# Attention backward on one Trainium2 core: dQ formed inside the loop from dS blocks transposed SBUF to SBUF, and dV with dK in one PSUM tile

## Chip, cores, metric

The kernel runs on one core of one Trainium2 chip. The metric is device time in microseconds, the median of several executions. Profiles are of one execution. Engines are written as in the profile: PE is the TensorE matmul, PEld its weight load, DVE is VectorE, ACT is ScalarE, POOL is GpSimd, SP is SyncE, which here only issues DMAs.

## The reference, cut to what matters

The reference computes a transformer block (2048 tokens, model width 512, 32 heads of width 16, feed-forward width 1792) and its gradients. Only the backward pass of the attention matters here. With E = exp(scores) and dOs, the output gradient divided by the softmax sum, the kernel computes for each head

```
S  = q k^T * 0.25           E  = exp(S)
D  = dOs v^T - delta        dS = E * D            (2048 x 2048 for each head)
dV = E^T dOs                dK = 0.25 * dS^T q
dQ = 0.25 * dS k            <- this one needs dS with k on the partitions
```

In the matmuls of this loop the contracted index lies on the partitions of both operands (psS in the profile: `32*128 32x512`, contracted over the 32 rows of a head). The loop produces dS with the query index on the partitions. That is right for dV and dK, which contract over queries. dQ contracts over keys, so it needs dS transposed.

## The kernel before

Four heads sit in 32-partition strips, so all matmuls of the loop use a part of the array (matmuls of other stages write `128*128` in the profile). psS and psD contract over 32 rows (row-tiled: the profile writes `32*128`). accV and accK contract over 128 rows into 32 columns (column-tiled: `128*32`). A scheduler orders the instructions of each engine at build time, from dependences and a cost model; the program order gives only priorities.

```python
# attention backward loop, cut; 8 head groups x 4 key chunks x 16 query tiles x 2 pairs of heads
for hp2 in range(2):
    psS_u = psu.tile([P, 2, 512], F32, name="psS_u", tag="pu")     # psu: 3 buffers of 128x1024 f32
    for hi in range(2):
        PE.matmul(psS_u[:, hi, :], qt_sb[32*hq:32*hq+32, ...], kt_sb[32*hq:32*hq+32, ...], ..., tile_position=(32*hq, 0))
    ACT.activation(E_u[:], psS_u[:], AF.Exp, scale=SCALE)
    psD_u = psu.tile([P, 2, 512], F32, name="psD_u", tag="pu")
    ...                                                             # psD_u <- dot_sb, vt_sb, row-tiled
    DVE.tensor_tensor(dS_u[:], psD_u[:], E_u[:], ALU.mult)
    for hi in range(2):
        PE.matmul(accV[32*hq:32*hq+32, :], dOs_tokpad[...], E_u[:, hi, :], ..., tile_position=(0, 32*hq))
        PE.matmul(accK[32*hq:32*hq+32, :], q_tok[...], dS_u[:, hi, :], ..., tile_position=(0, 32*hq))
    (POOL if (unit_ctr % 4) != 3 else SP).dma_start(out=dmadst, in_=dS_u[:])   # dS to DRAM
...
# a stage of its own for dQ, after the loop
for kt in range(TT):
    for hq in range(4):
        SP.dma_start(out=rd[:], in_=src, transpose=True)            # 2048 x 128 of dS, 512 KB
    for qc in range(QC):
        for hq in range(4):
            PE.matmul(accs[qc][32*hq:32*hq+32, :], k_tok[...], rds[hq][:, qc*512:(qc+1)*512], ..., tile_position=(0, 32*hq))
```

## Time and profile before

Before, the median is 6780 us (6771 to 6783). The first fence is from the page: busy tenths in 40 equal slices of the span for PE, the clock that TensorE was granted, and the DMA share.

```profile
PE   4799999997937668999999999999998666666676
...
PEclk8755555556968585555555555555555776767687
DMA  2200000001335543232333323232325999999932
```

The next is the table by stretches: length, busy time of each engine with the number of instructions in brackets, granted clock, DMA share and GB/s. The rows are the backward loop, the dQ stage, and the tail.

```profile
core 0: us, PE busy (x) PEld busy (x) DVE busy (x) ACT busy (x) POOL busy (x), PEclk, DMA share, GB/s
2544.00:5180.00 2636.00, 2541.46 (x8192) 443.87 (x8191) 1412.95 (x1280) 1049.99 (x1025) 547.99 (x768) 0.50 0.32 112
5180.00:6420.00 1240.00, 781.49 (x2036) 185.33 (x2037) 17.38 (x28) 0.00 (x0) 0.00 (x0) 0.70 1.18 220
6420.00:6740.00 320.00, 216.16 (x1058) 95.35 (x1075) 165.69 (x463) 28.99 (x52) 0.00 (x0) 0.76 0.25 82
```

In the loop PE is busy 96% of the time, and DVE and ACT about half. The granted clock is half of full speed throughout. In the dQ stage the DMA share is 1.18 (the packets' times add up to more than the span of the 16 engines, so packets overlap in time), and PE waits 461 us in all (478 waits) for transposed reads.

One period of the loop, PE alone, from the timeline. Columns: start, duration, engine, line, operation, tiles, shape, count.

```profile
3501.23 0.63 PE L700 MATMUL psD_u<-iv,ido 32*128 32x512 bf16 x1
3501.79 0.61 PE L711 MATMUL accK<-dS_u,q_tokH 128*32 128x512 bf16 x2
3502.33 0.60 PE L692 MATMUL psS_u<-ik,iq 32*128 32x512 bf16 x1
3502.86 0.61 PE L708 MATMUL accV<-E_u,dOs_tokpad 128*32 128x512 bf16 x2
3503.40 0.60 PE L692 MATMUL psS_u<-ik,iq 32*128 32x512 bf16 x1
3503.41 1.02 PE L700 MATMUL psD_u<-iv,ido 32*128 32x512 bf16 x2
```

Read the starts rather than the durations. Two matmuls on different strips start some 3 ns apart (the `x2` lines last 0.61 us, hardly more than one matmul). Two on the same strip start 0.40 us apart. From a row-tiled to a column-tiled matmul, or back, it takes 0.53 to 0.56 us (3501.23 to 3501.79, 3501.79 to 3502.33).

In what follows a **unit** is four heads, 128 queries, 512 keys; there are 512 units and one took 5.13 us. A **change** is a step between row- and column-tiled matmuls in the built PE order; there were 7.51 of them in a unit.

### The profile page before, as it was taken

The page shows a single profiled execution, that of the slowest core. Times are in us where ns is not written, and L with a number is a line of the kernel's source. Part 1 is how long each engine was busy: PE and PEld are TensorE (multiplying, and loading weights), DVE is VectorE, ACT ScalarE, POOL GpSimd, SP SyncE. Part 2 cuts the span into 40 slices and gives each one's busy share as a digit, 9 for nine tenths or more (in the row PEclk, how much of TensorE's full clock was granted, in tenths as well). Part 3 has the DMA queues.
Part 4 walks back from the last instruction along what each step waited for, and adds up shares of the span by engine and source line. Part 5 has one row for each costly group of instructions (what it writes and reads, how often), then busy time and mean ns, then how long its engine had stood idle before and what let it go on. Part 6 is the DMA issues. An engine that isn't in the chain of part 4 may idle for free. (4 is left out here: it accounts for less than half of the span.)

```text
span 6738.8 us, 51100 instructions
## 1 busy us (share of the span) xinstructions
PE 5556.9 (82%) x18807; PEld 1332.4 (20%) x18885; DVE 2278.3 (34%) x3423; ACT 2156.2 (32%) x2174; POOL 653.7 (10%) x920
## 2 busy tenths in 40 slices
PE   4799999997937668999999999999998666666676
PEld 2222222222313221111111111111111111111132
DVE  8300000006725034555555555555554000000044
ACT  0288888882000003433443433434432000000001
POOL 1000000000000021222222222222221000000000
PEclk8755555556968585555555555555555776767687
DMA  2200000001335543232333323232325999999932
GB/s 92 110 7 7 7 7 7 7 1 63 126 100 138 180 147 120 102 121 103 122 112 109 123 103 122 102 122 103 109 103 144 224 222 218 221 216 223 213 100 82
DMA packets 1327401, 764.37 MB, mean 113 GB/s; under 512 B 1144739, under 2 KB 1238439, under 8 KB 1325485
## 3 DMA queue, kind: packets, MB, share of 16 engines
q1 hardware_dynamic: 1259566, 531.42, 33.2%
q0 software_dynamic: 67584, 229.69, 9.9%
q8 instruction: 147, 2.41, 0.1%
q14 instruction: 104, 0.85, 0.0%
HBM read 126.51 MB, written 353.00 MB: 71 GB/s over the span
## 5 line engine op out<-in xcount | busy, mean ns | idle before, releaser
L704 DVE TENSOR_TENSOR dS_u<-psD_u,E_u 128x1024 bf16<-128x1024 f32 x1024 | 1248.2, 1224 | 1239.6 <-ACT E_u L696 1163.9
L696 ACT ACTIVATE E_u<-psS_u 128x1024 bf16<-128x1024 f32 x1024 | 1048.7, 1024 | 1578.6 <-PE psS_u L692 1578.6
L692 PE MATMUL psS_u<-ik,iq 32*128 32x512 bf16 x2048 | 1140.0, 602 | 31.1 <-ACT E_u L696 21.3
L303 ACT ACTIVATE ET<-psST 128x1024 bf16<-128x1024 f32 x1024 | 1047.1, 1025 | 227.8 <-PE psST L300 225.7
L700 PE MATMUL psD_u<-iv,ido 32*128 32x512 bf16 x2048 | 986.0, 616 | 37.1 <-ACT E_u L696 34.5
L300 PE MATMUL psST<-qt_sb,kt_sb 32*128 32x512 bf16 x2048 | 658.3, 603 | 17.3 <-DMA kt_sb<-KtP 17.3
L307 PE MATMUL oacc<-ET,vaug 128*32 128x512 bf16 x2048 | 625.7, 603 | 46.2 <-ACT ET L303 4.4
L711 PE MATMUL accK<-dS_u,q_tokH 128*32 128x512 bf16 x2048 | 624.6, 607 | 26.6 <-DVE dS_u L704 26.4
L708 PE MATMUL accV<-E_u,dOs_tokpad 128*32 128x512 bf16 x2048 | 599.7, 607 | 4.6
L783 ACT ACTIVATE dh1acc<-pdh_33667 128x512 f32<-128x512 f32 x1 | 0.6, 597 | 1262.5 <-PE pdh_33667 L780 1262.5
L743 PEld LDWEIGHTS <-k_tokI 128*32 128x32 bf16 x2048 | 186.2, 113 | 1065.1 <-issue 1010.8
L310 DVE COPY ostage<-oacc 128x512 f32<-128x512 f32 x32 | 22.1, 691 | 1083.7 <-PE oacc L307 1083.7
L692 PEld LDWEIGHTS <-iq 32*128 32x128 bf16 x2048 | 189.3, 98 | 860.9 <-issue 860.9
L711 PEld LDWEIGHTS <-q_tokH 128*32 128x32 bf16 x2048 | 114.1, 102 | 830.1 <-issue 829.8
L307 PEld LDWEIGHTS <-vaug 128*32 128x32 bf16 x2048 | 151.8, 102 | 466.2 <-issue 437.3
L300 PEld LDWEIGHTS <-kt_sb 32*128 32x128 bf16 x2048 | 111.6, 99 | 477.5 <-issue 477.5
L708 PEld LDWEIGHTS <-dOs_tokpad 128*32 128x32 bf16 x2048 | 110.0, 102 | 422.6 <-issue 420.0
L569 ACT ACTIVATE w1blk<-aw_0_13119 128x512 bf16<-128x512 f32 x1 | 0.6, 597 | 552.6 <-PE aw_0_13119 L565 552.6
L437 POOL MEMSET wT_pad<- 128x12288 bf16 x1 | 10.3, 10338 | 1702.7 <-DMA out_dram<-outq 1702.7
L489 PE MATMUL pds<-gfT,w2T 128*128 128x512 bf16 x219 | 55.5, 406 | 107.5 <-DVE dzT L492 78.8
L700 PEld LDWEIGHTS <-ido 32*128 32x128 bf16 x2048 | 127.4, 104 | 83.3 <-issue 77.2
L263 PE MATMUL ppad<-xn1T,wpadT 128*128 128x512 bf16 x376 | 97.8, 405 | 21.7 <-DVE stagep L266 16.2
(1483 smaller groups left out, 4521.4 us busy)
## 6 DMA issues: line engine op xcount, KB each, us to landing
dzld<-dztok_st POOLq DMA_DIRECT2D x32, 448.0 KB, 3.7
dzld<-dztok_st SPq DMA_DIRECT2D x32, 448.0 KB, 3.5
rT_st<-rT SPq DMA_DIRECT2D x4, 1792.0 KB
rtok_st<-rtok SPq DMA_DIRECT2D x16, 448.0 KB, 2.5
stok_st<-stok SPq DMA_DIRECT2D x16, 448.0 KB
rTb<-rT_st SPq DMA_DIRECT2D x4, 1792.0 KB
rtokb<-rtok_st SPq DMA_DIRECT2D x16, 448.0 KB, 4.1
dztok_st<-dztok SPq DMA_DIRECT2D x16, 448.0 KB
```

What stands on the lines that cost most here:

```text
L263: PE.matmul(pp[:], wpadT[:, ic, which, hg, :], h1T[:, ic, qc * 512:(qc + 1) * 512], start=(ic == 0), stop=(ic == DC - 1))
L300: PE.matmul(ps[:, hi, :], kt_sb[32 * hq:32 * hq + 32, kt * P:(kt + 1) * P], qt_sb[32 * hq:32 * hq + 32, qc * 512:(qc + 1) * 512], start=Tr ...
L303: ACT.activation(ET[:, 2 * pair:2 * pair + 2, :], ps[:], AF.Exp, scale=SCALE)
L307: PE.matmul(oacc[32 * hq:32 * hq + 32, :], lhsT, ET[:, hq, :], start=(kt == 0), stop=(kt == TT - 1), tile_position=(0, 32 * hq), skip_grou ...
L489: PE.matmul(pds[:], w2T[:, oc, fc * P:(fc + 1) * P], gfT[:, oc, qc * 512:(qc + 1) * 512], start=(oc == 0), stop=(oc == DC - 1))
L692: PE.matmul(psS_u[:, hi, :], qt_sb[32 * hq:32 * hq + 32, qt * P:(qt + 1) * P], kt_sb[32 * hq:32 * hq + 32, kb:kb + 512], start=True, stop= ...
L696: ACT.activation(E_u[:], psS_u[:], AF.Exp, scale=SCALE)
L700: PE.matmul(psD_u[:, hi, :], dot_sb[32 * hq:32 * hq + 32, qt * P:(qt + 1) * P], vt_sb[32 * hq:32 * hq + 32, kb:kb + 512], start=True, stop ...
L704: DVE.tensor_tensor(dS_u[:], psD_u[:], E_u[:], ALU.mult)
L708: PE.matmul(accV[32 * hq:32 * hq + 32, :], dOs_tokpad[:, qt, hg, 32 * hq:32 * hq + 32], E_u[:, hi, :], start=(qt == 0), stop=(qt == TT - 1 ...
L711: PE.matmul(accK[32 * hq:32 * hq + 32, :], q_tok[:, qt, h * DH:h * DH + 32], dS_u[:, hi, :], start=(qt == 0), stop=(qt == TT - 1), tile_po ...
L743: PE.matmul(accs[qc][32 * hq:32 * hq + 32, :], k_tok[:, kt, h * DH:h * DH + 32], rds[hq][:, qc * 512:(qc + 1) * 512], start=(kt == 0), sto ...
```

## The change

The intent is to remove the dS round trip through DRAM and the whole dQ stage. A DMA transposes each dS block from SBUF to SBUF. The program order puts dQ nine units later. To make room in PSUM for dQ's accumulator, dV and dK of four heads share one of 128x512 f32 (dV in rows 0 to 15 of a strip, dK in rows 16 to 31), which also lets dK and dV be emitted as groups of four heads.

```diff
+        def transpose_unit(u):
+            hg, qc, kc, qi = units[u]
+            if qi == 0:
+                dqt[hg, qc, kc] = tpool.tile([P, 16, 512], BF, name="dsT", tag="dsT")   # tpool: 2 buffers
+            SP.dma_start(out=dqt[hg, qc, kc][:, :, qi * P:(qi + 1) * P],
+                         in_=bst[u][1].rearrange("p h k -> p (h k)"), transpose=True)
+        def kv_quads(u):
...
+            for hq in range(4):
+                PE.matmul(acc[32 * hq:32 * hq + 32, :], st["qz"][:, qt, hq, :], dS_u[:, hq, :],
+                          start=(qi == 0), stop=False, tile_position=(0, 32 * hq), skip_group_check=True)
+            for hq in range(4):
+                PE.matmul(acc[32 * hq:32 * hq + DH, :], dOs_tok[...], E_u[:, hq, :],
+                          start=False, stop=(qi == 3), tile_position=(0, 32 * hq), skip_group_check=True)
...
+        LAG = 6
+        for u in range(NU + LAG + 4):
+            if u < NU:
+                score_pair(u, 0)            # psS, exp, psD, dS of heads 0, 1
+            if 1 <= u <= NU:
+                kv_quads(u - 1)
+            if u < NU:
+                score_pair(u, 1)            # heads 2, 3
+                transpose_unit(u)
+            v = u - LAG - 3
+            if 0 <= v < NU:
+                dq_quad((hg, qc, kc), qi)   # four matmuls into dqacc
-    (the loop and the dQ stage shown above, and the DRAM tiles of dS)
```

Also: dV and dK are flushed from PSUM every four units and summed in SBUF by ACT and POOL. k and q are scaled beforehand. The tail transposes and multiplies two packed tiles instead of three. x is loaded again for the tail to make room in SBUF.

More of the change, by code (lines that the diff above doesn't have):

```diff
@@ L73 @@
         SP.dma_start(out=auxsel[32 * j + 16:32 * j + 17, :], in_=onesf[0:1, 0:1])
-    x0_tok = persist.tile([P, TT, D], BF, name="x0_tok")
+    x0pool = tc.alloc_tile_pool(name="x0pool", bufs=1, side="right")
+    x0_tok = x0pool.tile([P, TT, D], BF, name="x0_tok")
     SP.dma_start(out=x0_tok[:], in_=x_dram)
@@ L105 @@
     dQtP = dram.tile([HG, P, n], BF, name="dQtP")
-    dKtP = dram.tile([HG, P, n], BF, name="dKtP")
-    dVtP = dram.tile([HG, P, n], BF, name="dVtP")
-    dS_st = [[dram.tile([4, n, 512], BF, name=f"dS_{hg}_{kc4}") for kc4 in range(QC)] for hg in range(HG)]
+    dVKtP = dram.tile([HG, P, n], BF, name="dVKtP")
     with ExitStack() as ph:
@@ L432 @@
     x1pool.release()
+    x0pool.release()
     bwdw = ctx.enter_context(tc.tile_pool(name="bwdw", bufs=1))
-    wT_pad = bwdw.tile([P, 24, D], BF, name="wT_pad")
+    wT_pad = bwdw.tile([P, 16, D], BF, name="wT_pad")
     POOL.memset(wT_pad[:], 0.0)
@@ L460 @@
                     r0 = (hg % 2) * 64 + hq * DH
-                    SP.dma_start(out=wT_pad[32 * hq:32 * hq + DH, t3 * 8 + hg, :], in_=tmpT[r0:r0 + DH, :])
+                    o0 = 32 * hq + (DH if t3 == 1 else 0)
+                    SP.dma_start(out=wT_pad[o0:o0 + DH, (0 if t3 == 0 else 8) + hg, :], in_=tmpT[r0:r0 + DH, :])
         for oc in range(DC):
@@ L590 @@
     qpool = tc.alloc_tile_pool(name="qpool", bufs=1)
-    q_tok = qpool.tile([P, TT, QPAD], BF, name="q_tokH")
-    SP.dma_start(out=q_tok[:], in_=q_st[:])
-    dOs_tokpad = qpool.tile([P, TT, HG, P], BF, name="dOs_tokpad")
+    dOs_tok = qpool.tile([P, TT, D], BF, name="dOs_tok")
+    hpool = tc.alloc_tile_pool(name="hpool", bufs=1)
+    dOs_tokpad = hpool.tile([P, TT, HG, P], BF, name="dOs_tokpad")
     POOL.memset(dOs_tokpad[:], 0.0)
-    hpool = tc.alloc_tile_pool(name="hpool", bufs=1)
     woT = hpool.tile([P, DC, D], BF, name="woT")
@@ L629 @@
                 DVE.tensor_tensor(dst, src, rb, ALU.mult)
+                POOL.tensor_copy(dOs_tok[:, t, :].rearrange("q (g h d) -> q g h d", g=HG, h=4), dst)
                 O_t = wk.tile([P, D], BF, name="O_t", tag="O_t")
@@ L661 @@
     hpool.release()
+    KS_tok = qpool.tile([P, TT, QPAD], BF, name="KS_tok")
+    SP.dma_start(out=KS_tok[:], in_=k_st[:])
+    DVE.tensor_scalar(KS_tok[:], KS_tok[:], SCALE, None, ALU.mult)
+    qz = [qpool.tile([P, TT, 4, 32], BF, name=f"qz{i}") for i in range(2)]
+    for i in range(2):
+        POOL.memset(qz[i][:], 0.0)
     with ExitStack() as ph:
@@ L665 @@
         ework = ph.enter_context(tc.tile_pool(name="phIe", bufs=3))
+        tpool = ph.enter_context(tc.tile_pool(name="phIt", bufs=2))
         stg = ph.enter_context(tc.tile_pool(name="phIg", bufs=2))
@@ L668 @@
         psu = ph.enter_context(tc.tile_pool(name="psIu", bufs=3, space=bass.MemoryType.PSUM))
-        psvk = ph.enter_context(tc.tile_pool(name="psIvk", bufs=1, space=bass.MemoryType.PSUM))
-        unit_ctr = 0
-        for hg in range(HG):
-            qt_sb = strm.tile([P, n], BF, name="iq", tag="iq")
-            SP.dma_start(out=qt_sb[:], in_=QtP[hg])
-            kt_sb = strm.tile([P, n], BF, name="ik", tag="ik")
-            SP.dma_start(out=kt_sb[:], in_=KtP[hg])
-            vt_sb = strm.tile([P, n], BF, name="iv", tag="iv")
-            SP.dma_start(out=vt_sb[:], in_=VtP[hg])
-            dot_sb = strm.tile([P, n], BF, name="ido", tag="ido")
-            SP.dma_start(out=dot_sb[:], in_=dOtP[hg])
-            dVstage = stg.tile([P, n], BF, name="dVstage", tag="dVstage")
-            dKstage = stg.tile([P, n], BF, name="dKstage", tag="dKstage")
-            for kc4 in range(QC):
-                kb = kc4 * 512
-                accV = psvk.tile([P, 512], F32, name="accV", tag="accV")
-                accK = psvk.tile([P, 512], F32, name="accK", tag="accK")
-                for qt in range(TT):
-                    for hp2 in range(2):
-                        hqs = (2 * hp2, 2 * hp2 + 1)
-                        psS_u = psu.tile([P, 2, 512], F32, name="psS_u", tag="pu")
-                        for hi in range(2):
-                            hq = hqs[hi]
-                            PE.matmul(psS_u[:, hi, :], qt_sb[32 * hq:32 * hq + 32, qt * P:(qt + 1) * P],
-                                      kt_sb[32 * hq:32 * hq + 32, kb:kb + 512],
-                                      start=True, stop=True, tile_position=(32 * hq, 0))
-                        E_u = ework.tile([P, 2, 512], BF, name="E_u", tag="E_u")
-                        ACT.activation(E_u[:], psS_u[:], AF.Exp, scale=SCALE)
-                        psD_u = psu.tile([P, 2, 512], F32, name="psD_u", tag="pu")
-                        for hi in range(2):
-                            hq = hqs[hi]
-                            PE.matmul(psD_u[:, hi, :], dot_sb[32 * hq:32 * hq + 32, qt * P:(qt + 1) * P],
-                                      vt_sb[32 * hq:32 * hq + 32, kb:kb + 512],
-                                      start=True, stop=True, tile_position=(32 * hq, 0))
-                        dS_u = ework.tile([P, 2, 512], BF, name="dS_u", tag="dS_u", bufs=6)
-                        DVE.tensor_tensor(dS_u[:], psD_u[:], E_u[:], ALU.mult)
-                        for hi in range(2):
-                            hq = hqs[hi]
-                            h = hg * 4 + hq
-                            PE.matmul(accV[32 * hq:32 * hq + 32, :], dOs_tokpad[:, qt, hg, 32 * hq:32 * hq + 32],
-                                      E_u[:, hi, :], start=(qt == 0), stop=(qt == TT - 1),
-                                      tile_position=(0, 32 * hq), skip_group_check=True)
-                            PE.matmul(accK[32 * hq:32 * hq + 32, :], q_tok[:, qt, h * DH:h * DH + 32],
-                                      dS_u[:, hi, :], start=(qt == 0), stop=(qt == TT - 1),
-                                      tile_position=(0, 32 * hq), skip_group_check=True)
-                        dmadst = dS_st[hg][kc4][2 * hp2:2 * hp2 + 2, qt * P:(qt + 1) * P, :].rearrange("h q k -> q h k")
-                        (POOL if (unit_ctr % 4) != 3 else SP).dma_start(out=dmadst, in_=dS_u[:])
-                        unit_ctr += 1
-                for hq in range(4):
-                    DVE.tensor_copy(dVstage[32 * hq:32 * hq + 32, kb:kb + 512], accV[32 * hq:32 * hq + 32, :])
-                    DVE.tensor_scalar(dKstage[32 * hq:32 * hq + 32, kb:kb + 512], accK[32 * hq:32 * hq + 32, :],
-                                      SCALE, None, ALU.mult)
-            SP.dma_start(out=dVtP[hg], in_=dVstage[:])
-            SP.dma_start(out=dKtP[hg], in_=dKstage[:])
@@ L724 @@
-    with ExitStack() as ph:
-        kpool = ph.enter_context(tc.tile_pool(name="phI2k", bufs=1))
-        io = ph.enter_context(tc.tile_pool(name="phI2io", bufs=8))
-        stg = ph.enter_context(tc.tile_pool(name="phI2s", bufs=2))
-        psq = ph.enter_context(tc.tile_pool(name="psI2", bufs=2, space=bass.MemoryType.PSUM))
-        k_tok = kpool.tile([P, TT, QPAD], BF, name="k_tokI")
-        SP.dma_start(out=k_tok[:], in_=k_st[:])
-        for hg in range(HG):
-            accs = [psq.tile([P, 512], F32, name=f"dqacc{qc}", tag=f"dqacc{qc}") for qc in range(QC)]
-            for kt in range(TT):
-                rds = []
-                for hq in range(4):
-                    rd = io.tile([P, n], BF, name="dsT_rd", tag="dsT_rd")
-                    src = dS_st[hg][kt // 4][hq:hq + 1, :, (kt % 4) * P:(kt % 4 + 1) * P].rearrange("h q k -> (h q) k")
-                    SP.dma_start(out=rd[:], in_=src, transpose=True)
-                    rds.append(rd)
-                for qc in range(QC):
-                    for hq in range(4):
-                        h = hg * 4 + hq
-                        PE.matmul(accs[qc][32 * hq:32 * hq + 32, :], k_tok[:, kt, h * DH:h * DH + 32],
-                                  rds[hq][:, qc * 512:(qc + 1) * 512], start=(kt == 0), stop=(kt == TT - 1),
-                                  tile_position=(0, 32 * hq), skip_group_check=True)
-            dQstage = stg.tile([P, n], BF, name="dQstage", tag="dQstage")
-            for qc in range(QC):
-                DVE.tensor_scalar(dQstage[:, qc * 512:(qc + 1) * 512], accs[qc][:], SCALE, None, ALU.mult)
-            SP.dma_start(out=dQtP[hg], in_=dQstage[:])
@@ new lines, with load_head @@
+        psa = ph.enter_context(tc.tile_pool(name="psIa", bufs=1, space=bass.MemoryType.PSUM))
+        units = [(hg, qc, kc, qi) for hg in range(HG) for qc in range(QC) for kc in range(QC) for qi in range(4)]
+        hst, bst, dqt = {}, {}, {}
+        def load_head(hg):
+            st = {}
+            for key, src in (("q", QtP), ("k", KtP), ("v", VtP), ("do", dOtP)):
+                st[key] = strm.tile([P, n], BF, name=f"i{key}", tag=f"i{key}")
+                SP.dma_start(out=st[key][:], in_=src[hg])
+            st["qz"] = qz[hg % 2]
+            qs = strm.tile([P, TT, 64], BF, name="iqs", tag="iqs")
+            ACT.dma_start(out=qs[:], in_=q_st[:, :, hg * 64:(hg + 1) * 64])
+            POOL.tensor_scalar(qz[hg % 2][:, :, :, DH:2 * DH], qs.rearrange("p t (h d) -> p t h d", h=4),
+                               SCALE, None, ALU.mult)
+            st["acc"] = stg.tile([P, n], F32, name="dVKacc", tag="dVKacc", bufs=1)
+            st["dq"] = stg.tile([P, n], BF, name="dQst", tag="dQst")
+            hst[hg] = st
@@ new lines, in score_pair @@
+        def score_pair(u, pair):
+            hg, qc, kc, qi = units[u]
+            st = hst[hg]
+            qt = qc * 4 + qi
+            if pair == 0:
+                bst[u] = (ework.tile([P, 4, 512], BF, name="E_u", tag="E_u"),
+                          ework.tile([P, 4, 512], BF, name="dS_u", tag="dS_u", bufs=4))
+            E_u, dS_u = bst[u]
+            psS = psu.tile([P, 2, 512], F32, name="psS_u", tag="pu")
+            for hi in range(2):
+                r = 32 * (2 * pair + hi)
+                PE.matmul(psS[:, hi, :], st["q"][r:r + 32, qt * P:(qt + 1) * P], st["k"][r:r + 32, kc * 512:kc * 512 + 512],
+                          start=True, stop=True, tile_position=(r, 0))
+            ACT.activation(E_u[:, 2 * pair:2 * pair + 2, :], psS[:], AF.Exp, scale=SCALE)
+            psD = psu.tile([P, 2, 512], F32, name="psD_u", tag="pu")
+            for hi in range(2):
+                r = 32 * (2 * pair + hi)
+                PE.matmul(psD[:, hi, :], st["do"][r:r + 32, qt * P:(qt + 1) * P], st["v"][r:r + 32, kc * 512:kc * 512 + 512],
+                          start=True, stop=True, tile_position=(r, 0))
+            DVE.tensor_tensor(dS_u[:, 2 * pair:2 * pair + 2, :], psD[:], E_u[:, 2 * pair:2 * pair + 2, :], ALU.mult)
@@ new lines, in transpose_unit @@
+        def transpose_unit(u):
+            hg, qc, kc, qi = units[u]
+            if qi == 0:
+                dqt[hg, qc, kc] = tpool.tile([P, 16, 512], BF, name="dsT", tag="dsT")
+            SP.dma_start(out=dqt[hg, qc, kc][:, :, qi * P:(qi + 1) * P],
+                         in_=bst[u][1].rearrange("p h k -> p (h k)"), transpose=True)
+        cur = {}
+        def kv_quads(u):
+            hg, qc, kc, qi = units[u]
+            st = hst[hg]
+            qt = qc * 4 + qi
+            E_u, dS_u = bst.pop(u)
+            if qi == 0:
+                cur["vk"] = psa.tile([P, 512], F32, name="accVK", tag="accVK")
+            acc = cur["vk"]
+            for hq in range(4):
+                PE.matmul(acc[32 * hq:32 * hq + 32, :], st["qz"][:, qt, hq, :], dS_u[:, hq, :],
+                          start=(qi == 0), stop=False, tile_position=(0, 32 * hq), skip_group_check=True)
+            for hq in range(4):
+                PE.matmul(acc[32 * hq:32 * hq + DH, :], dOs_tok[:, qt, (hg * 4 + hq) * DH:(hg * 4 + hq + 1) * DH], E_u[:, hq, :],
+                          start=False, stop=(qi == 3), tile_position=(0, 32 * hq), skip_group_check=True)
+            if qi == 3:
+                dst = st["acc"][:, kc * 512:(kc + 1) * 512]
+                if qc == 0:
+                    ACT.activation(dst, acc[:], AF.Identity)
+                else:
+                    tmp = wk.tile([P, 512], F32, name="vktmp", tag="vktmp")
+                    ACT.activation(tmp[:], acc[:], AF.Identity)
+                    POOL.tensor_tensor(dst, dst, tmp[:], ALU.add)
+                if qc == QC - 1 and kc == QC - 1:
+                    vkb = stg.tile([P, n], BF, name="vkb", tag="vkb", bufs=1)
+                    POOL.tensor_copy(vkb[:], st["acc"][:])
+                    SP.dma_start(out=dVKtP[hg], in_=vkb[:])
@@ new lines, in dq_quad @@
+        def dq_quad(b, kt):
+            hg, qc, kc = b
+            if kc == 0 and kt == 0:
+                cur["dq"] = psa.tile([P, 512], F32, name="dqacc", tag="dqacc")
+            acc = cur["dq"]
+            tT = dqt[b]
+            for hq in range(4):
+                h = hg * 4 + hq
+                PE.matmul(acc[32 * hq:32 * hq + 32, :], KS_tok[:, kc * 4 + kt, h * DH:h * DH + 32], tT[:, hq * 4 + kt, :],
+                          start=(kc == 0 and kt == 0), stop=(kc == QC - 1 and kt == 3),
+                          tile_position=(0, 32 * hq), skip_group_check=True)
+            if kt == 3:
+                del dqt[b]
+                if kc == QC - 1:
+                    ACT.activation(hst[hg]["dq"][:, qc * 512:(qc + 1) * 512], acc[:], AF.Identity)
+                    if qc == QC - 1:
+                        SP.dma_start(out=dQtP[hg], in_=hst[hg]["dq"][:])
@@ new lines @@
+        LAG = 6
+        NU = len(units)
+        load_head(0)
+        for u in range(NU + LAG + 4):
+            if u < NU:
+                if units[u][1:] == (0, 2, 0) and units[u][0] + 1 < HG:
+                    load_head(units[u][0] + 1)
+                score_pair(u, 0)
[6 more added lines that the diff above has]
+            if 0 <= v < NU:
+                hg, qc, kc, qi = units[v]
+                dq_quad((hg, qc, kc), qi)
@@ L759 @@
         dh1acc = bigJ2.tile([P, TT, D], F32, name="dh1acc")
+        x0_tok = bigJ2.tile([P, TT, D], BF, name="x0_tokJ")
+        SP.dma_start(out=x0_tok[:], in_=x_dram)
         with ExitStack() as ph2:
@@ L762 @@
             psd = ph2.enter_context(tc.tile_pool(name="psJd", bufs=2, space=bass.MemoryType.PSUM))
-            srcs = (dQtP, dKtP, dVtP)
+            srcs = (dQtP, dVKtP)
             for hg in range(HG):
                 xs = []
-                for t3 in range(3):
+                for t3 in range(2):
                     xt = stgJ.tile([P, n], BF, name=f"xst{t3}", tag=f"xst{t3}")
@@ L770 @@
                 for qt in range(TT):
-                    pt = pst.tile([P, 3, P], BF, name="ptq", tag="ptq")
+                    pt = pst.tile([P, 2, P], BF, name="ptq", tag="ptq")
+                    for t3 in range(2):
+                        PE.transpose(pt[:, t3, :], xs[t3][:, qt * P:(qt + 1) * P], identb[:])
                     for t3 in range(3):
-                        PE.transpose(pt[:, t3, :], xs[t3][:, qt * P:(qt + 1) * P], identb[:])
-                    dst = dqkv_tok[:, qt, :].rearrange("q (t g hd) -> q t g hd", t=3, g=HG)[:, :, hg, :]
-                    dst = dst.rearrange("q t (h d) -> q t h d", h=4)
-                    srcv = pt.rearrange("q t (h c) -> q t h c", h=4)[:, :, :, 0:DH]
-                    DVE.tensor_copy(dst, srcv)
+                        dst = dqkv_tok[:, qt, t3 * D + hg * 64:t3 * D + (hg + 1) * 64].rearrange("q (h d) -> q h d", h=4)
+                        srcv = pt[:, 0 if t3 == 0 else 1, :].rearrange("q (h c) -> q h c", h=4)
+                        srcv = srcv[:, :, DH:2 * DH] if t3 == 1 else srcv[:, :, 0:DH]
+                        if t3 == 0:
+                            ACT.activation(dst, srcv, AF.Identity)
+                        else:
+                            DVE.tensor_copy(dst, srcv)
                     pd = psd.tile([P, D], F32, name="pdh1", tag="pdh1")
-                    for t3 in range(3):
+                    for t3 in range(2):
                         PE.matmul(pd[:], xs[t3][:, qt * P:(qt + 1) * P], wT_pad[:, t3 * 8 + hg, :],
-                                  start=(t3 == 0), stop=(t3 == 2))
+                                  start=(t3 == 0), stop=(t3 == 1))
                     if hg == 0:
```

## The prediction

> **What bounds the kernel now.** The per-stretch table of engine busy time splits the 6738.8 us span: before attention backward 2544 us; the backward loop 2636 us (2544 to 5180), PE 2541 us busy, DVE 1413, ACT 1050, granted clock 0.50, DMA share 0.32; the separate dQ stage 1240 us (5180 to 6420), PE 781, clock 0.70, DMA share above 1, 220 GB/s; the tail 320 us.
>
> The loop is bound by PE order. The timeline shows a period of 2.57 us for each pair of heads (1024 pairs). Eight matmuls start in about five slots: row-tiled psS (one head), column-tiled accV x2, psS with psD, psD, accK x2, psS again. Matmuls on different row or column groups start 3 ns apart; on the same group 0.40 us apart; a change between row and column tiling costs 0.54 us. [...] ACT (1.02 us) and DVE (1.22 us) are half idle.
>
> The dQ stage is bound by the transposing reads: 512 of 512 KB, 2.42 us each, in 256-byte packets; its matmuls wait for them, and their releases gate the next reads.
>
> **What the change does.** The dQ stage goes (-1240 us), with the dS stores. Per unit (four heads, 128 q x 512 k; 512 units; now 5.14 us) the loop keeps 16 matmuls and takes over 4 for dQ. dK and dV come as groups of four heads on four column groups, so 20 matmuls fit 7 slots: psS 0.54, psD 0.40, dK 0.54, dV 0.40, psS 0.54, psD 0.40, dQ 0.55: an estimate of 3.4 us if the built order keeps the groups together and the clock stays at 0.50. ACT needs 2.05 us plus evictions (128 + 32 of about 0.6 us, 0.2 us a unit), DVE 2.45 us: neither binds.
>
> One 512 KB transpose per unit goes SBUF to SBUF. At 2.42 us (issue in the trace: median 2.17 us) it fits. [...]
>
> I don't expect 3.4 us. The order now takes 2.57 us where an ideal grouping of its eight matmuls would take about 1.9. Also only two dsT blocks and four dS buffers exist: dQ of block b-2 must finish before the transposes of block b, dS holds its buffer until its transpose lands, and dQ is queued nine units late. A stall of some 4-5 us per block of four units is likely. I estimate 4.3 us a unit: loop about 2200 us.
>
> The tail loses one of three transposes and matmuls per tile: about -25 us; reload of x and scaling of k: some us back.
>
> **Sum:** 6780 - 1240 - 436 - 25 = about 5080 us. Range 4650 (3.5 us a unit) to 5600 (5.3). Chances: faster 0.93, same 0.02, slower 0.05.
>
> **What would show it.** Right: no dQ stage; loop length 1800 to 2700 us; q1 packets no longer read DRAM there; transposes landing in under 5 us; PE busiest in the loop, clock near 0.5; dK/dV matmuls starting four together; HBM written down by about 270 MB. Wrong: PE idle with "DMA dsT" or "DVE dS" as releaser and DVE waiting for transposes, which would mean the transposes pace the loop.
>
> **What would make it wrong.** No SBUF-to-SBUF transpose is in the trace: if one takes over 5 us the loop becomes DMA-bound; at 8 us everything is lost. [...] The scheduler splitting the groups. [...]

Four passages that no trace of this case showed when it was recorded are cut from the forecast, at the marks: one on changes of tiling, one on the rate of transposes, and two risks, of which one was that the clock might be higher. None is a term of the sum, which stays at 6780 - 1240 - 436 - 25 = about 5080 us. The 2.42 us of a transpose are the dQ stage's 1240 us over its 512 transposes (512 KB each, so 216 GB/s). The limits of 5 and 8 us are estimates from the same table: a unit of the loop took 5.14 us, and the loop with the dQ stage 3876 us, 7.6 us a unit.

## The result

The median fell from 6780 to 5016 us (5011 to 5024). The ratio is 0.7404, with a 95% interval of 0.7393 to 0.7414. Ratios here and below are the mean time of one kernel's runs over that of the kernel before in the same rounds, so they are not quite the ratios of the medians quoted. Executions over 1.5% slower than the fastest of the same kernel are left out of the means. Two experiments are compared by dividing their ratios.

The slices of the page, after:

```profile
PE   4789999999997872866579999998989999989766
...
PEclk7865555555555886966855565666565655666687
DMA  3220000000001243365467867777686877677513
```

The table by stretches, after: the loop, with dQ in it, and the tail.

```profile
core 0: us, PE busy (x) PEld busy (x) DVE busy (x) ACT busy (x) POOL busy (x), PEclk, DMA share, GB/s
2575.00:4725.00 2150.00, 1944.39 (x10234) 368.38 (x10233) 1222.26 (x1024) 1099.93 (x1185) 152.85 (x110) 0.61 0.73 136
4725.00:5010.00 285.00, 184.42 (x794) 74.92 (x808) 162.02 (x587) 55.27 (x180) 0.00 (x0) 0.76 0.23 76
```

The dQ stage of 1240 us is gone. The loop is 486 us shorter although it does 2048 matmuls more. The tail is 35 us shorter. What comes before the loop is about 30 us longer. By the page, HBM writes fell from 353 to 80 MB.

The waits of PE and SP in the new loop (who waited for whom; total, times, longest). The first fence is PE waiting for a transpose, the second is the queue that issues the transposes.

```profile
PE dqacc L762 <- DMA dsT<-dS_u: 9.8, 6, 3.8
```

```profile
SPq L722 <- DVE dS_u L716: 1658.6, 507, 6.7
```

PE waited only 10 us for transposes in the whole loop. The queue waited almost only for fresh dS, not for the release of a dsT block by dQ. So the stall that the prediction expected isn't there. Section 6 of the page gives the transposes' time from issue to landing, 4.3 us:

```profile
dsT<-dS_u SPq DMA_TRANSPOSE x512, 4.3
```

A piece of the new timeline, PE alone, at the lower clock:

```profile
3503.73 0.61 PE L714 MATMUL psD_u<-iv,ido 32*128 32x512 bf16 x2 [0.75 <-ACT E_u L710]
3504.27 0.61 PE L736 MATMUL accVK<-dS_u,qz_14655 128*32 128x512 bf16 x2
3504.82 0.60 PE L708 MATMUL psS_u<-ik,iq 32*128 32x512 bf16 x1
3505.35 0.61 PE L736 MATMUL accVK<-dS_u,qz_14655 128*32 128x512 bf16 x2
3505.36 1.03 PE L739 MATMUL accVK<-E_u,dOs_tok 128*16 128x512 bf16 x4
3506.32 0.60 PE L708 MATMUL psS_u<-ik,iq 32*128 32x512 bf16 x1
3506.32 1.02 PE L714 MATMUL psD_u<-iv,ido 32*128 32x512 bf16 x2
3507.28 0.61 PE L762 MATMUL dqacc<-dsT,KS_tok 128*32 128x512 bf16 x1
```

The dV group runs as four (`x4`). The dK group is torn into two pairs with a lone psS between them, and one dQ matmul stands alone between row-tiled ones. Each such tear costs two changes. The clock of 0.61 is a mean: in the traces of the kernel before and of this one, every record of the granted clock is 1.0 (full) or 0.5 (half).

The following table is worked out from the start times of the matmuls in the traces: the time from each start to the next, summed by what lies between them. It covers the loops of the two kernels and of three experiments told below. The long steps at the two ends of a loop are left out; all matmul records of these loops are in the traces.

| loop | changes | us at changes | mean | us, row to row | us, column to column | sum | PEclk |
|---|---|---|---|---|---|---|---|
| before | 3843 | 2095 | 0.545 | 466 | 66 | 2627 | 0.50 |
| changed | 2263 | 1189 | 0.525 | 453 | 496 | 2138 | 0.61 |
| e1_group_only | 1955 | 1108 | 0.567 | 484 | 373 | 1965 | 0.50 |
| e6_order | 2033 | 1111 | 0.546 | 470 | 217 | 1798 | 0.50 |
| e8_fill4 | 2033 | 736 | 0.362 | 517 | 258 | 1511 | 0.91 |

Of the loop, 906 us less goes to changes, and 417 us more to steps inside runs of one kind.

### The profile page after: what moved, and what is told of

It reads as the page before. It is cut to its first block, busy times and chain, and to the rows that moved or that the text cites. A ratio compares the mean times of both kernels' runs of the same rounds, so it can differ in the third digit from the quotient of the medians.

```text
span 5010.0 us, 48266 instructions
## 1 busy us (share of the span) xinstructions
PE 4158.7 (83%) x18556; PEld 1052.9 (21%) x18629; DVE 2069.8 (41%) x3264; ACT 2232.8 (45%) x2462; POOL 274.0 (5%) x282
## 4 chain that ended last, share of the span: by engine, by line
PE 33%; ACT 8%; DVE 5%; DMA 3%; issue 3%; SPq 1%; POOL 0%; ACTq 0%; DVEq 0%; POOLq 0%
PE psS_u L708 8%; PE accVK L736 8%; ACT E_u L710 7%; PE psD_u L714 6%; PE dqacc L762 5%; PE accVK L739 4%; DVE dS_u L716 3%; DMA dsT<-dS_u 1%; SPq L919 1%; DMA stld<-stok_st 0%; DVE dh1acc L831 0%; DVE dqkv_tok L823 0%; DMA out_dram<-w2blk 0%; ACT vktmp L747 0%; POOL dOs_tokpad L595 0%
## 5 line engine op out<-in xcount | busy, mean ns | idle before, releaser
L716 DVE TENSOR_TENSOR dS_u<-psD_u,E_u 128x1024 bf16<-128x1024 f32 x1024 | 1222.3, 1222 | 965.6 <-ACT E_u L710 780.2
L710 ACT ACTIVATE E_u<-psS_u 128x1024 bf16<-128x1024 f32 x1024 | 1018.6, 1023 | 886.3 <-PE psS_u L708 881.4
L714 PE MATMUL psD_u<-iv,ido 32*128 32x512 bf16 x2048 | 643.3, 540 | 107.7 <-ACT E_u L710 91.9
L708 PE MATMUL psS_u<-ik,iq 32*128 32x512 bf16 x2048 | 601.6, 532 | 22.5 <-ACT E_u L710 14.8
L739 PE MATMUL accVK<-E_u,dOs_tok 128*16 128x512 bf16 x2048 | 462.9, 554 | 0.0
L762 PE MATMUL dqacc<-dsT,KS_tok 128*32 128x512 bf16 x2048 | 427.9, 605 | 12.5 <-DMA dsT<-dS_u 9.8
L736 PE MATMUL accVK<-dS_u,qz_14655 128*32 128x512 bf16 x1024 | 316.8, 543 | 35.5 <-DVE dS_u L716 35.3
L736 PE MATMUL accVK<-dS_u,qz_14654 128*32 128x512 bf16 x1024 | 303.7, 557 | 26.8 <-DVE dS_u L716 26.7
L708 PEld LDWEIGHTS <-iq 32*128 32x128 bf16 x2048 | 126.1, 96 | 663.8 <-issue 650.3
L748 POOL TENSOR_TENSOR dVKacc<-dVKacc,vktmp 128x512 f32<-128x512 f32 x96 | 121.3, 1264 | 1910.0 <-ACT vktmp L747 1910.0
L736 PEld LDWEIGHTS <-qz_14655 128*32 128x32 bf16 x1024 | 59.1, 99 | 312.4 <-issue 311.9
L736 PEld LDWEIGHTS <-qz_14654 128*32 128x32 bf16 x1024 | 56.1, 99 | 295.8 <-issue 295.8
```

Of the source, the lines that this page charges most:

```text
L708: PE.matmul(psS[:, hi, :], st["q"][r:r + 32, qt * P:(qt + 1) * P], st["k"][r:r + 32, kc * 512:kc * 512 + 512], start=True, stop=True, tile ...
L710: ACT.activation(E_u[:, 2 * pair:2 * pair + 2, :], psS[:], AF.Exp, scale=SCALE)
L714: PE.matmul(psD[:, hi, :], st["do"][r:r + 32, qt * P:(qt + 1) * P], st["v"][r:r + 32, kc * 512:kc * 512 + 512], start=True, stop=True, til ...
L716: DVE.tensor_tensor(dS_u[:, 2 * pair:2 * pair + 2, :], psD[:], E_u[:, 2 * pair:2 * pair + 2, :], ALU.mult)
L736: PE.matmul(acc[32 * hq:32 * hq + 32, :], st["qz"][:, qt, hq, :], dS_u[:, hq, :], start=(qi == 0), stop=False, tile_position=(0, 32 * hq), ...
L739: PE.matmul(acc[32 * hq:32 * hq + DH, :], dOs_tok[:, qt, (hg * 4 + hq) * DH:(hg * 4 + hq + 1) * DH], E_u[:, hq, :], start=False, stop=(qi ...
```

## The experiments

Theory A: the loop is paced by PE's built order, that is by the number of changes. Theory B, which the prediction leaned on: transposes and the buffers they hold pace the changed loop. Two more theories, C and D, about the clock came up on the way. Twelve kernels ran.

### Grouping alone

The edit takes the changed kernel, puts the store of dS to DRAM and the old dQ stage back, and keeps the new loop order.

```diff
-            SP.dma_start(out=dqt[hg, qc, kc][:, :, qi * P:(qi + 1) * P], in_=..., transpose=True)
+            for pair in range(2):
+                (POOL if (2 * u + pair) % 4 != 3 else SP).dma_start(out=dmadst, in_=bst[u][1][:, 2 * pair:2 * pair + 2, :])
```

> The loop of the changed kernel, but dS goes to DRAM and the separate dQ stage is kept: only the grouping of dK and dV by four heads is left of the change. Theory A (the loop is paced by TensorE's order: each change between row- and column-tiled matmuls costs about 0.53 us, built order 3.82 changes a unit against 7.51 before and 4.42 after): about 3.5 us a unit, loop about 1790 us, dQ stage about 1240, total about 5890. Theory B (transposes and their buffers pace the changed loop): a loop without them falls to about 2.9 us a unit, total about 5560.

It took 6077 us, ratio 0.8991. The loop and the dQ stage by the table of stretches:

```profile
2575.00:4530.00 1955.00, 1738.13 (x8148) 309.13 (x8144) 1202.25 (x1019) 1070.26 (x1145) 700.44 (x873) 0.50 0.42 146
4535.00:5790.00 1255.00, 791.06 (x2039) 187.47 (x2036) 17.38 (x28) 0.00 (x0) 0.60 (x1) 0.69 1.18 217
```

The loop fell from 2627 to 1965 us at the same clock of 0.50 and with the same 16 matmuls a unit. The built order has half the changes, 3.82 a unit instead of 7.51, and the time at changes fell by 987 us. This is the cleanest evidence for A. The loop was still about 175 us longer than A's estimate: steps inside runs of one kind cost 325 us more than before, mostly steps of over 0.6 us. B's 5560 is refuted. One limit of the run: it keeps the rest of the new loop too (the shared accumulator of dV and dK, flushed every four units by ACT and POOL, and the new program order), so "grouping" stands for the new loop without dQ.

So grouping alone brings 10%, and the rest of the change, on top of it, another 18% (0.7404 / 0.8991 = 0.823): the loop takes in the dQ matmuls for about 170 us, and a stage of 1255 us goes.

### dQ in the loop, without the grouping

```diff
-            if 1 <= u <= NU:
-                kv_quads(u - 1)
+                kv_pair(u, 0)        # dK h0, dV h0, dK h1, dV h1
                 score_pair(u, 1)
+                kv_pair(u, 1)
                 transpose_unit(u)
```

> The changed kernel with dQ in the loop, but dK and dV emitted pair by pair again. Built order 5.88 changes a unit. Theory A: about 4.9 us a unit instead of 4.18, total about 5400. Theory B: the transposes pace it, so about 5020 as before this edit.

The three fast executions took 5128 to 5185 us, ratio 0.7639, which is 3.2% slower than the changed kernel; a fourth, the profiled one, was slow (5207 us). Neither number was met; A's direction was right at less than half its size. It isn't the old order either: dK and dV of a pair now stand together (5.88 changes, not 7.51). The grouping by four is therefore worth 10% without dQ in the loop, and only 3% with it against this order.

The trace says what hides in the 3%, with the caution that it is one execution, and a slow one. Two stretches of its loop:

```profile
2590.00:2780.00 190.00, 156.52 (x1114) 42.72 (x1112) 134.15 (x112) 121.84 (x128) 13.92 (x11) 1.00 0.87 154
2810.00:4900.00 2090.00, 2068.24 (x8791) 323.91 (x8787) 1076.07 (x880) 969.62 (x1016) 130.08 (x94) 0.51 0.64 119
```

At two DVE instructions a unit, a unit takes 3.39 us in the first stretch, at full clock, and 4.75 us in the second, at half. The order is not what changed: by the start times, 113 blocks of four units run the same sequence of 80 matmuls, 14 of them at full clock (3.43 us a unit) and 99 at half (4.78 us, near A's 4.9). The clock fell where the first head group ends and, but for some 10 us now and then, did not come back. So the 3% compares two kernels at the clocks that they happened to get, and not their orders alone.

### No transposes, and transposes that nobody reads

Both give a wrong result. In the first, dQ reads a fixed tile of real data and nothing is transposed. In the second the transposes run, but dQ still reads the fixed tile.

```diff
-            SP.dma_start(out=dqt[hg, qc, kc][...], in_=..., transpose=True)
+            dqt[hg, qc, kc] = dsT0                # first run
-            tT = dqt[b]
+            tT = dsT0                             # second run; the transposes stay
```

> Wrong result on purpose: no transposes at all, dQ reads one fixed tile of real data, so neither their DMA time nor the waits for their buffers exist. Theory A: built order 4.19 changes a unit, so 4.0 to 4.1 us a unit, total 4920 to 4970. Theory B: the stall of 4 to 5 us per block of four units goes, about 3.2 us a unit, total about 4500.

> Wrong result on purpose: the transposes run as in the changed kernel but dQ reads a fixed tile of real data, so no matmul waits for one and the built order (4.17 changes a unit) is that of the run without transposes (4.19). If the 350 us that leaving out the transposes gained came from the order and from waits for them: about 4670. If they came from the DMA traffic beside the matmuls (granted clock 0.69 without it, 0.61 with it): about 5000.

They took 4668 us (ratio 0.6908) and 4685 us (0.6936). The first fell between what A and B said. The DMA traffic beside the matmuls costs next to nothing: with all the transposes running, the second run differs by 0.4% from the first, and in the last four of the eight head groups a unit takes 3.85 us in both.

But what these runs gained over the changed kernel (6 to 7%) can't be put down to waits for transposes, because neither keeps its order. A dQ that reads a fixed tile depends on no transpose, and the scheduler moved all of dQ forward. In the first run (the line of the dQ matmuls, with their first and last start, then two stretches of the loop):

```profile
L762 PE MATMUL dqacc<-dsT,KS_tok x2048: 377/389/634, 2555.4 to 3260.3; 128*32 128x512 bf16 x187
2570.00:3250.00 680.00, 619.88 (x5448) 158.91 (x5448) 514.72 (x432) 471.45 (x519) 62.01 (x44) 1.00 0.06 19
3300.00:4370.00 1070.00, 951.10 (x4451) 169.31 (x4450) 656.64 (x557) 584.54 (x627) 83.27 (x61) 0.50 0.02 9
```

Up to 3260 us there are some nine dQ matmuls a unit instead of four, the clock is full and a unit takes 3.15 us. After that there is no dQ, the clock is half and a unit takes 3.84 us, as in the loop of "Grouping alone" (3.83 us). The second run has the same two parts, so the mean clocks of 0.69 and 0.68 over the two loops hide them. How much of the gain is order and how much is clock was not separated. That dQ must wait for landed transposes is not itself a cost of this size: the kernels of "PE's order by hand" below keep that dependence and are as fast.

### More dS buffers

```diff
-                          ework.tile([P, 4, 512], BF, name="dS_u", tag="dS_u", bufs=4))
+                          ework.tile([P, 4, 512], BF, name="dS_u", tag="dS_u", bufs=6))
```

> Six dS buffers instead of four (and one dQ staging buffer instead of two, to make room), same built PE order. Theory A: nothing, 5016 us within 1%. Theory B: the predicted stall of 4 to 5 us per block goes, 128 blocks, total about 4450 to 4600.

5013 us, ratio 0.7412 against 0.7404: nothing. The predicted stall of 4 to 5 us for each block of four units does not exist. A third dsT block was not tried; that the two blocks hold nothing up rests on the waits above, where the queue never waits for dQ to release one.

### Every block transposed twice

```diff
+            again = tpool.tile([P, 16, P], BF, name="again", tag="again")
+            SP.dma_start(out=again[:], in_=bst[u][1].rearrange("p h k -> p (h k)"), transpose=True)
```

> Each dS is transposed twice, the second time into a tile that nobody reads; nothing else changes but one dQ staging buffer fewer. The DMA share of the changed loop is 0.73 at 4.18 us a unit, that is about 3.05 us of all 16 engines for one transpose. If that share is real occupancy, two need about 6.1 us a unit, the loop becomes DMA-bound at about 3100 us and the total rises to about 5950. If the transposes have slack to spare for another (2.42 us each by the old dQ stage, 4.84 for two), about 2500 us of loop and 5350 in total. If transposes did not matter at all, 5016.

It took 5557 us, ratio 0.8226, between the first two numbers. A unit took 5.24 us, that is 2.62 us for each transpose. The queue is full: SP waits 92 us for dS, where it waited 1659 us before. Now transposes do pace the loop, as its waits show:

```profile
DVE dS_u L716 <- DMA again<-dS_u: 1264.4, 429, 9.2
PE psD_u L714 <- DVE dS_u L716: 543.8, 356, 3.8
```

DVE can't write dS because an older dS is still being transposed, and PE waits for DVE. This is the chain that the prediction feared, and it needs twice the DMA work to appear. It also gives the size that the estimate lacked: one SBUF-to-SBUF transpose of 512 KB takes 2.62 us in a full queue, against 2.42 us for one from DRAM. The DMA share of 0.73 times 4.18 us is 3.05 us, so the share overstates how full the engines are.

### PE's order by hand

The first of two kernels pins PE to the program order. psD of heads 2 and 3 of the last unit stands beside psS of heads 0 and 1, on four strips; likewise psD of heads 0 and 1 beside psS of heads 2 and 3. dQ follows six units late. The second has the same program order but leaves PE to the scheduler.

```diff
+        def mm(*a, **k):
+            ins = PE.matmul(*a, **k)
+            tc.keep_in_program_order(ins)          # left out in e6b_order_free
...
+            grad_pair(u - 1, 1); transpose_unit(u - 1)   # psD, dS of heads 2, 3
+            score_pair(u, 0)                             # psS, exp of heads 0, 1
+            kv_quads(u - 2)
+            grad_pair(u, 0)
+            score_pair(u, 1)
+            dq_quad(...)                                 # of unit u - 6
```

> Same work as the changed kernel, but TensorE's order is fixed by hand: psD of heads 2 and 3 of the last unit beside psS of heads 0 and 1 of this one (four row groups), dK and dV of four heads, psD of heads 0 and 1 beside psS of heads 2 and 3, dQ of four heads, with dQ six units late. Theory A (order): 3.97 changes a unit but only two row slots instead of four; estimate 2.6 us of matmul slots, bound by the chain psS, exp, buffer, psS, exp, buffer at 3.4 us a unit: loop 1740, total about 4620. Theory B (transposes): no gain, about 5016.

> The same emission order as the hand-ordered kernel, but left to the scheduler (4.03 changes a unit). Theory A: some of the gain, about 4800. Theory B: about 5016.

They took 4658 us (ratio 0.6896) and 4638 us (0.6863). Both are faster than the changed kernel by 7%, with correct results and all transposes in place. One unit of the pinned kernel, PE alone:

```profile
3500.83 0.61 PE L681 MATMUL psS_u<-ik,iq 32*128 32x512 bf16 x2 [0.29 <-DVE dS_u L726]
3501.37 0.62 PE L681 MATMUL accVK<-dS_u,qz 128*32 128x512 bf16 x4
3501.77 0.65 PE L681 MATMUL accVK<-E_u,dOs_tok 128*16 128x512 bf16 x4
3502.34 0.60 PE L681 MATMUL psD_u<-iv,ido 32*128 32x512 bf16 x2
3502.35 0.60 PE L681 MATMUL psS_u<-ik,iq 32*128 32x512 bf16 x2
3502.89 0.62 PE L681 MATMUL dqacc<-dsT,KS_tok 128*32 128x512 bf16 x4
3503.44 0.60 PE L681 MATMUL psD_u<-iv,ido 32*128 32x512 bf16 x2
```

```profile
2575.00:4350.00 1775.00, 1624.03 (x10096) 280.35 (x10093) 1190.79 (x1010) 1115.52 (x1168) 148.53 (x107) 0.50 0.88 162
```

All groups are whole. A unit takes 3.50 us, near the 3.4 estimated. PE's waits are nearly all for a PSUM buffer: psS waits for DVE to finish dS of the pair before (135 us in 474 waits, from 2600 to 4300 us; all others together 8 us). But the clock stayed at 0.50 from end to end, where the changed kernel had 0.61 and the free order 0.73. The free order needs more steps but runs about half of its matmuls at full clock, and comes out equal. So the clock had become the question.

### Useless matmuls

Theory C, a guess to be tested: the clock follows how much of the time 128-row matmuls stream. Theory D: it doesn't depend on that. After each dQ group, four or eight matmuls with zero weights are added. They add zero to the dQ accumulator, so results stay right.

```diff
+            if not (kc == QC - 1 and kt == 3):
+                for z in range(4):                       # 8 in e8_fill8
+                    hq = z % 4
+                    mm(acc[32 * hq:32 * hq + 32, :], zw[:], tT[:, hq * 4 + kt, :], start=False, stop=False,
+                       tile_position=(0, 32 * hq), skip_group_check=True)
```

> The hand-ordered kernel plus useless work: after each dQ group four more column-tiled matmuls with zero weights add nothing to the dQ accumulator (result stays right). The hand-ordered loop ran at a granted clock of 0.50 throughout, with about 0.5 us of slack in its 3.5 us unit; the changed kernel's loop had 0.61, the free order 0.73. Theory C (the clock follows how much of the time 128-row matmuls stream): the added 0.4 us a unit lifts the clock, the slots halve, a unit takes about 2.9 us, total about 4370. Theory D (the clock doesn't depend on that): the clock stays at 0.50 and the unit grows by 0.1 to 0.4 us, total 4700 to 4870.

> The same with eight zero-weight matmuls after each dQ group. Theory C: the clock is raised more surely; about 3.0 us a unit, total about 4400. Theory D: clock 0.50, a unit of 4.1 to 4.4 us, total 4950 to 5100.

They took 4371 us (ratio 0.6455) and 4400 us (0.6496), both correct. Adding 1920 useless matmuls made the pinned kernel 6.4% faster. The table of stretches and one unit of the timeline, for four:

```profile
2575.00:4070.00 1495.00, 1314.42 (x12036) 307.00 (x12035) 1229.18 (x1015) 1105.87 (x1172) 149.79 (x108) 0.91 1.09 193
```

```profile
3500.26 0.39 PE L683 MATMUL psS_u<-ik,iq 32*128 32x512 bf16 x2 [0.20 <-DVE dS_u L728]
3500.58 0.40 PE L683 MATMUL dqacc<-dsT,KS_tok 128*32 128x512 bf16 x4
3500.80 0.39 PE L683 MATMUL dqacc<-dsT,zw 128*32 128x512 bf16 x4
3501.12 0.39 PE L683 MATMUL psD_u<-iv,ido 32*128 32x512 bf16 x2
3501.56 0.39 PE L683 MATMUL psS_u<-ik,iq 32*128 32x512 bf16 x2
3501.88 0.40 PE L683 MATMUL accVK<-dS_u,qz 128*32 128x512 bf16 x4
```

The built order is the same as without the filling but for the added lines. The clock went from 0.50 to 0.91, a matmul lasts 0.39 us instead of 0.61, and a change costs 0.31 us in most cases. A unit takes 2.95 us. Now DVE is busy 82% of the loop, and the DMA share is 1.09.

Two last runs put the same filling into the two original kernels, with the order left to the scheduler.

```diff
+                        for z in range(4):               # e11: the kernel before, after dK of each pair
+                            hq = hqs[z % 2]
+                            if qt < TT - 1:
+                                PE.matmul(accK[32 * hq:32 * hq + 32, :], zw[:], dS_u[:, z % 2, :], start=False, stop=False, ...)
```

> The changed kernel with four zero-weight matmuls after each dQ group, order left to the scheduler, which scatters them: 5.29 changes a unit instead of 4.42. Theory C (the clock follows how much of the time 128-row matmuls stream): clock in the loop from 0.61 to 0.8 or more, changes cost 0.31 to 0.35 us instead of 0.53, total 4600 to 4800 in spite of more work and more changes. Theory D: clock as it was, total about 5200 to 5300.

> The kernel before with four zero-weight column-tiled matmuls a pair of heads after dK, built order 6.49 changes a unit against 7.51. Theory C: its loop, at a clock of 0.50 and 5.14 us a unit, gets a higher clock and falls below 4.5 us a unit, total under 6450. Theory D: clock 0.50, no shorter: about 6500 to 6800 by the order alone.

The filled changed kernel took 4681 to 4736 us in its three fast executions (a fourth, 4829 us, was slow), ratio 0.6949, so 6.1% faster than the changed kernel. The filled kernel before took 6309 us, ratio 0.9327. The loop of the second:

```profile
2550.00:4715.00 2165.00, 1869.96 (x12019) 559.08 (x12016) 1389.50 (x1271) 1046.31 (x1023) 549.25 (x767) 0.89 0.39 134
```

Its clock went from 0.50 to 0.89 and its loop from 2627 to about 2170 us, for 3840 useless matmuls. Part of that may be order, since the built order had 6.49 changes a unit instead of 7.51. Theory D's numbers were missed in all four runs. Shown, then, is that with column-tiled matmuls added the granted clock of the loop was higher in these kernels (0.91 instead of 0.50 in the pinned one, 0.85 instead of 0.61 in the changed one, 0.89 instead of 0.50 in the one before), and that the filling paid for itself; the pinned kernel shows it without a change of order. Not shown is what decides the clock: all fillings were column-tiled, of 128 rows, and placed beside other column-tiled work. Real column-tiled work went with a full clock too: nine dQ matmuls a unit at 1.00, none at 0.50, in the run without transposes. Nor is the clock fixed by the built order alone. In the run without the grouping one sequence of matmuls ran at full clock first and at half clock afterwards; neither C nor D foresaw that, and what made the clock fall there stays open.

## Why the prediction was right or wrong

- **The dQ stage goes, 1240 us.** Right; nothing of it was seen to come back as DMA contention. Leaving out all transposes while dQ reads a fixed tile differs by 0.4% from running them unread, though in an order of its own.
- **The loop has fewer, wider steps.** Right in mechanism. The new loop without dQ was shorter by a quarter at an unchanged clock. The "7 slots, 3.4 us" of the prediction was reached only when the order was pinned: 3.50 us at clock 0.50.
- **"A stall of some 4-5 us per block of four units is likely."** This step failed. More dS buffers changed nothing, PE waited 10 us in all for transposes, and the queue waited for dS. The stall was derived from the program's nine units between a score and its dQ. The scheduler didn't keep them: in the trace the first dQ group of a block starts about 6 units after its scores and the last about 4.5, so a dsT block comes free long before it is wanted.
- **"I estimate 4.3 us a unit."** Measured: 4.18. The number held for another reason, which is luck: a stall that isn't there made up for costs that were not counted. In its place stand torn groups, which the prediction named only as a risk (4.42 changes a unit instead of 4, and 496 us of steps inside column runs, where whole groups would need one step of 0.40 us a unit, some 205 us in all), less a higher clock.
- **The clock "near 0.5".** It rose to 0.61, and the prediction named that only as a risk. It is no small matter: in the pinned kernel the clock of 0.91 that came with the useless work made it 6% faster than at 0.50.
- **The transpose at 2.42 us.** Measured 2.62 us, that is 200 GB/s for 512 KB, and 4.3 us from issue to landing.
- **The tail, -25 us.** Measured -35 us, with about 30 us more before the loop.

The fastest kernel found is the pinned order with four zero-weight matmuls a unit: 4371 us, ratio 0.6455, 13% faster than the changed kernel (0.6455 / 0.7404 = 0.872). Its unit of 2.95 us lies near two floors that the runs show: 2.62 us for the transpose and 2.45 us for two DVE multiplications.

## What to carry to other kernels

When matmuls use strips of the array, count the changes of tiling in the built PE order: here each cost about 0.54 us at half clock and 0.31 us at full clock, against 0.40 and 0.22 us for a second matmul on the same strip, and halving their number, with the new loop's shared accumulator, was worth 10% with no matmul removed. Look at the granted clock beside PE's busy share, because here a PE that was 96% busy ran at a clock of 0.50 throughout, the pinned order left it at 0.50, and four zero-weight matmuls a unit went with 0.91. Look at the clock stretch by stretch, too: a mean of 0.69 was a loop at full clock followed by one at half. The transposing DMA between SBUF tiles was nearly free beside the tiled matmuls (0.4%) while its 2.62 us for 512 KB fitted under a unit's compute of 3.85 us; twice as many set the unit at 5.24 us. Check that by doubling the transposes rather than by the DMA share, which overstated them here.
